# Start of an attention and two-layer kernel: the written order of blocks 0 and 1, with the queue of a store and the buffers of an output

## The chip, the cores and the metric

The kernel runs on one core of one Trainium2 chip. The metric is the time of one execution in microseconds (us); lower is better.

## The reference

All arrays are of 32-bit floats but the weights, which come as 64-bit floats.

```python
def _attn_ref(q, k, v):                    # [8, 8, 576, 64] each
    k_p = k.reshape(B, H, Sp, pool, D).mean(axis=3)   # pool = 8: 72 keys
    v_p = v.reshape(B, H, Sp, pool, D).mean(axis=3)
    scores = scale * np.matmul(q, k_p.transpose(0, 1, 3, 2))
    scores = scores - np.max(scores, axis=-1, keepdims=True)
    attn = np.exp(scores)
    attn = attn / (np.sum(attn, axis=-1, keepdims=True) + 1e-09)
    return np.matmul(attn, v_p)

x = attn_out.transpose(0, 2, 1, 3).reshape(4608, 512)
h = np.maximum(x @ w_in, 0.0)              # w_in 512 x 2048, w_out 2048 x 512
x = h * h @ w_out
h = x @ w2_in
out = np.maximum(0.01 * h, h) @ w2_out
```

## The kernel before, in words

**Tiles.** The 4608 tokens are worked in nine blocks of T = 512. A block's first product has FC = 16 chunks of 128 of the 2048 inner columns, its second product four result tiles (KC = 4 of 128 columns). Phase 0 runs attention and the first pair of weights over all blocks and leaves the result in DRAM (x2); phase 1 runs the second pair. A product is done in three passes, with each factor as the sum of two 32-bit terms: high by high, high by low, low by high. So one chunk of a first product is 4 x 3 = 12 matrix products of 512 columns.

**Weights.** A matrix of weights comes in pieces n = 0 to 15 of 1 MB (0 to 7 of w_in, 8 to 15 of w_out; each w_in piece makes two chunks). `w1.load(n)` (L268, on SP's queue) brings the 64-bit words. `w1.do(letter, n)` then turns them into the two terms, in five steps: a, the exponents (ScalarE, L218); b, the first bits (VectorE, L222 and L225); c, the low term (VectorE, L236 and L239); d, the high term (VectorE L280, and a ScalarE copy, L283); e, the low rest (VectorE, L287).

**The start.** `start()` walks a list of words, START: K, Q and V load keys, queries and values, i loads a weight piece, a to e are the conversion steps, q, k, s, n, p, x, v, m and w are attention steps (transpose of queries, pooled keys, scores with their exponentials, normalization, transpose of the probabilities, pooling of block 1's keys, pooling of values, their split, their placing). Then the values of block 0 are multiplied (L687 to L690).

**First products of blocks 0 and 1** (`first_products`, 32 units u, 16 per block). A unit multiplies one chunk into one of four PSUM banks in turn (L850), converts a weight piece (`conversion`, a piece per two units), takes relu and square on ScalarE (L860, L861) and stores the result to a DRAM buffer, `mid` (L1038). Units 0 to 15 also hold the attention of block 1, dealt out by `second_attention`: lists pe[u] of what is written ahead of a unit's products and dve[u] of what is written behind its relu (normalization L610 to L613, copies of a remainder L621, transposes of probabilities L644 and L650, their splitting L654 and L663, values L672 and L673). `loads_of(u)` deals out the loads. Results of block 0 go through tiles "r" (three buffers); those of block 1 through a ring of pieces of xh and xl.

**Second products of blocks 0 and 1** (`second_products`, 32 units). The stored results are read back six units ahead (`mid_load`, L1048), split into two terms on VectorE (`in_parts`, L866 and L867) and multiplied (L893) into the four banks. The last two pieces of w_out, n = 14 and 15, are converted here, and the attention of block 2 is dealt out among the units. At a block's end `finish` copies the four banks to tiles in turn by ScalarE (L910, m = 0 and 2) and VectorE (L908, m = 1 and 3), and SP stores them (L911).

**The other blocks** run one after the other (`run`): first products, relu, second products of one block, with the next block's attention between.

The order on every engine is the order in which the code is written. DMAs on SP's queue are issued in written order, and a DMA waits, ahead of those behind it, for what it needs. The buffers of a kind are handed out in turn: "r", "st" and "raw" have three, "gh" and "gl" two.

Of the kernel before, what the change touches and what calls it, by code (L numbers as in the profile page):

```python
# [43 lines left out]
def attention_relu2_leaky_kernel(  # L44
# [12 lines left out]
    nc = tc.nc  # L57
    B, H, S, D = q.shape
    NT, DM = out.shape
# [10 lines left out]
    T = 512  # L70
# [3 lines left out]


    START = (
        "K0 Q0 Q1 Q2 Q3 V0 i0 K1 i1 i2 Q4 Q5 i3 "
        "q0 q1 k0 s0 q2 s1 q3 n0 s2 v0 n1 s3 p0 m0 n2 p1 x1 n3 a0 b0 p2 c0 w0 d0 p3 a1 e0"
    ).split()

    pool = ctx.enter_context(tc.tile_pool(name="sb", bufs=1))
# [548 lines left out]
    def p_products(i, blk, t0):  # L630

        s = sc.pop(i)[0]
        flat = s.rearrange("p h k -> p (h k)")
        if blk not in pt:
            pt[blk] = (
                sb([P, NP, T], F32R, "pth"),
                sb([P, NP, T], F32R, "ptl"),
                sb([P, 2, T], F32R, "ptr"),
            )
        ph, pl, pr = pt[blk]  # L640
        o = i * P - t0
        ps = bank()
        for cc in range(NP):
            nc.tensor.transpose(  # L644
                ps[:, cc * P : (cc + 1) * P], flat[:, cc * PAIR : cc * PAIR + P], ident
            )

        pr_ps = bank()
        for g in range(2):
            nc.tensor.transpose(  # L650
                pr_ps[:RROWS, g * P : (g + 1) * P], prems[i % 2][:, g, :], ident
            )
        view = ps.rearrange("p (c t) -> p c t", c=NP)
        nc.scalar.copy(ph[:, :, o : o + P], view)  # L654
        last = pr_ps[:, : 2 * P].rearrange("p (c t) -> p c t", c=2)
        nc.scalar.copy(pr[:RROWS, :, o : o + P], last[:RROWS])
        low = slice(4 * REM, RROWS)

        def rest():
            for out, src in ((pl, view), (pr[low], last[low])):  # L660
                at = out[:, :, o : o + P]
                hi = ph if out is pl else pr[low]
                nc.vector.tensor_tensor(  # L663
                    out=at, in0=src, in1=f32(hi[:, :, o : o + P]), op=ALU.subtract
                )

        return rest
# [36 lines left out]
    def load_q(i):  # L704
        if i in first_tiles:
            load_home(("q", i), q_load(i))
        else:
            load_to(("q", i), q_load(i), "raw")
# [191 lines left out]

    def finish(ph, t0, acc):

        tags = ("st", "raw") if ph or t0 + T == NT else ("st", "st")
        to = x2[:, t0 : t0 + T] if ph == 0 else out[t0 : t0 + T, :]
        for m in range(KC if ph == 0 else T // P):
            st = sb([P, T if ph == 0 else DM], F32, tags[m % 2])
            if m % 2:
                nc.vector.tensor_copy(st, acc[m])  # L908
            else:
                nc.scalar.copy(st, acc[m])  # L910
            nc.sync.dma_start(out=to[m * P : (m + 1) * P, :], in_=st)  # L911
# [55 lines left out]
    def second_attention():  # L967


        pe, dve = [[] for _ in range(FC)], [[] for _ in range(FC)]  # L970
        blk, b = 1, 1
        dve[0] += [pooled_late[0], lambda: k_mask(b)]
        pe[1].append(lambda: k_transpose(b))

        def both(u, fn):
            pe[u].append(lambda: dve[u].extend(fn()))

        for j, i in enumerate(range(T // P, 2 * T // P)):
            u = 1 + 3 * j
            pe[u].append(lambda i=i: (q_transpose(i), taken(("q", i))))  # L980
            both(u + 1, lambda i=i: score_products(i))
            dve[u + 2].append(lambda i=i: normalize(i))
            both(u + 3, lambda i=i: [p_products(i, blk, T)])
        for n, (what, c) in enumerate([("v", c) for c in range(NP)] + [("rem", c) for c in range(2)]):
            both(5 + n, lambda what=what, c=c: [v_tile_pe(b, what, c)])
        dve[11].append(lambda: v_split(b))
        turn = value_steps(blk, T)
        pe[12].append(turn[0])

        def placed():  # L990
            built.add(b)
            v_place(b)

        pe[13].append(placed)
        pe[15].append(turn[1])
        return pe, dve

    def loads_of(u):

        if u == 1:  # L1000
            for c in range(NP):
                load_to(("v", 1, c), v_load(1, c), ("st", "st", "st", "gh")[c])
            for c in range(2):
                load_to(("rem", 1, c), rem_load(1, c), "gl")
        if u in (5, 8):
            load_q(6 + (u == 8))
        if u % 2 == 0 and 4 + u // 2 < FC - 2:
            w1.load(4 + u // 2)

    def conversion(u):  # L1010

# [8 lines left out]
    def first_products():  # L1020
        pe, dve = second_attention()
        for u in range(2 * FC):
            blk, c = divmod(u, FC)
            for fn in pe[u] if blk == 0 else ():
                fn()
            ps = first(blk, c)
            if u < 2 * FC - 6:
                conversion(u)
            if u == FC:
                ring.extend(t[:, i] for t in x_tiles(dt=F32) for i in range(KC))  # L1030
            r = ring[c % len(ring)] if blk else sb([P, T], F32, "r")
            relu2(r, ps)
            if u % 2 == 0 and u < 2 * FC - 8:
                w1.do("a", u // 2 + 2)
            for fn in dve[u] if blk == 0 else ():
                fn()
            loads_of(u)
            nc.sync.dma_start(out=mid[blk, c], in_=r)  # L1038
            if blk and c >= FC - AHEAD:
                mid_load(c - FC + AHEAD)  # L1040

# [8 lines left out]
    def second_products():  # L1050
        steps, turn = all_steps[2], value_steps(2, 2 * T)
        n_units, done = 2 * FC, 0
        for n in (FC - 2, FC - 1):
            w1.load(n)
        load()
        g = in_parts(mids.pop(0))
        for u in range(n_units):
            blk, c = divmod(u, FC)
            if c == 0:
                acc = [acc_bank(m) for m in range(KC)]  # L1060
            mid_load(u + AHEAD)
            if u + 1 < n_units:
                g_next = in_parts(mids.pop(u + 1))
            if u >= n_units - 2:
                turn.pop(0)()
            second(0, c, acc, g)
            for n in (FC - 2, FC - 1):
                at = u - 2 * (n - FC + 2)
                if 0 <= at < 3:
                    w1.do(("a", "bc", "de")[at], n)  # L1070
            upto = len(steps) * (u + 1) // (n_units - 2)
            while done < min(upto, len(steps)):
                steps[done]()
                done += 1
            if u >= FC // 2:
                w2.tick()
            if c == FC - 1:
                finish(0, blk * T, acc)
            g = g_next
# [69 lines left out]
```

## Time and profile before

| | us |
|---|---|
| median of three runs | 1848.42 |
| the three runs | 1848.19, 1848.42, 1849.64 |
| the profiled execution | 1846.85 |
| its span in the profile | 1845.1 |

Of the span TensorE (PE) is busy 1756.7 us (95%), VectorE (DVE) 942.5 (51%), ScalarE (ACT) 517.5 (28%). The chain of work that ended last lies to 86% on PE. The mean granted clock of PE is 0.977 of full speed. In the page's 40 slices of 46 us, PE's busy tenths begin 5 7 7 8 7 8 8 and are 9 from the eighth slice on.

The rows below have these forms. A row of waits names the waiting engine, tile and line, then the engine, tile and line that ended the wait, then the total in us, how often, and the longest. A row of a timeline has start and length in us, engine, line, operation, what is written and read, and in brackets the idle time of the engine just before and what ended it. A row of windows has the stretch, its length, each engine's busy us with its number of instructions, the granted clock (1.00 is full speed), the share of the DMA engines in use, and GB/s.

### The profile page before, as it was taken

What the parts mean: (1) busy time and instruction counts of PE and PEld (TensorE: products, weight loads), DVE (VectorE), ACT (ScalarE), POOL (GpSimd) and SP (SyncE); (2) the same over time, 40 slices, a digit from 0 to 9 for tenths busy, and PEclk for the clock granted to TensorE, in tenths of its full rate; (3) what the DMA queues carried; (4) which work ended last, traced back from release to release, by engine and by line L of the source; (5) the groups of instructions that cost most, each with busy time, mean ns of one, the idle gap of its engine ahead of it and who ended that gap; (6) DMA issues with size and microseconds to landing.
All of it is one profiled execution on the core that took longest, in us unless ns stands there. A gap on an engine that the chain in (4) does not pass through costs nothing.

```text
span 1845.1 us, 20649 instructions
## 1 busy us (share of the span) xinstructions
PE 1756.7 (95%) x8024; PEld 1454.6 (79%) x8024; DVE 942.5 (51%) x1687; ACT 517.5 (28%) x1283; POOL 0.7 (0%) x5
## 2 busy tenths in 40 slices
PE   5778788999999999999999999999999999999999
PEld 4666567888878888888888888888888888888887
DVE  6666476766766667676442234343434343434333
ACT  3455411333344343433342211111111111111111
POOL 0000000000000000000000000000000000000000
PEclk9789898999999999999999999999999999999999
DMA  8343544232323223232005511010101010101000
GB/s 233 111 137 117 185 140 158 94 100 93 100 83 114 92 92 125 86 108 92 29 1 205 204 47 46 1 46 1 46 1 46 1 46 1 46 1 46 0 24 23
DMA packets 97633, 144.01 MB, mean 78 GB/s; under 512 B 42624, under 2 KB 42752, under 8 KB 95488
## 3 DMA queue, kind: packets, MB, share of 16 engines
q1 hardware_dynamic: 97536, 142.70, 23.4%
q8 instruction: 63, 1.03, 0.2%
q14 instruction: 34, 0.28, 0.0%
HBM read 98.64 MB, written 44.04 MB: 77 GB/s over the span
## 4 chain that ended last, share of the span: by engine, by line
PE 86%; DVE 8%; ACT 3%; DMA 1%; issue 1%; SPq 1%; DVEq 0%; ACTq 0%
PE acc L893 40%; PE ps L850 38%; PE acc L850 2%; PE ps L578 2%; PE ps L545 1%; DVE val L225 1%; PE ps L644 1%; DVE val L280 1%; DVE xl L673 0%; DVE gl L867 0%; PE ps L688 0%; DMA raw<-in_q 0%; DVE val L222 0%; DMA wo<-in_v 0%; PE ps L687 0%
## 5 line engine op out<-in xcount | busy, mean ns | idle before, releaser
L850 PE MATMUL ps<-xh,wi 128*128 128x512 f32 x2048 | 673.9, 391 | 0.0
L850 PEld LDWEIGHTS ps<-xh,wi 128*128 128x128 f32 x2048 | 384.7, 188 | 79.6 <-issue 0.2
L850 PE MATMUL ps<-xl,wi 128*128 128x512 f32 x1024 | 398.8, 389 | 0.0
L876 DVE SCALAR_TENSOR_TENSOR r<-r 128x512 f32<-128x512 f32 x144 | 99.7, 693 | 461.6 <-ACT r L875 461.6
L893 PE MATMUL acc<-gh,wo 128*128 128x512 f32 x1152 | 300.1, 399 | 12.8 <-DVE st L908 7.0
L893 PE MATMUL acc<-wo,gh 128*128 128x512 f32 x1152 | 288.9, 389 | 0.0
L875 ACT COPY r<-ps 128x512 f32<-128x512 f32 x144 | 84.5, 587 | 655.6 <-PE ps L850 655.6
L893 PEld LDWEIGHTS acc<-gh,wo 128*128 128x128 f32 x1152 | 216.0, 191 | 60.1 <-DVE st L908 8.2
L893 PEld LDWEIGHTS acc<-wo,gh 128*128 128x128 f32 x1152 | 216.3, 188 | 44.9
L850 PEld LDWEIGHTS ps<-xl,wi 128*128 128x128 f32 x1024 | 192.4, 188 | 39.1
L866 DVE CAST gh<-r 128x512 fp32r<-128x512 f32 x256 | 109.2, 427 | 220.7 <-ACT r L861 206.4
L867 DVE TENSOR_TENSOR gl<-r,gh 128x512 fp32r<-128x512 f32 x256 | 177.3, 692 | 21.8 <-DVE gh L866 0.9
L893 PE MATMUL acc<-gl,wo 128*128 128x512 f32 x576 | 160.4, 393 | 0.0
L893 PE MATMUL acc<-wo,gl 128*128 128x512 f32 x576 | 158.3, 389 | 0.0
L860 ACT ACTIVATE r<-ps 128x512 f32<-128x512 f32 x112 | 67.7, 605 | 234.1 <-PE ps L850 234.1
L893 PEld LDWEIGHTS acc<-gl,wo 128*128 128x128 f32 x576 | 109.3, 190 | 23.4
L893 PEld LDWEIGHTS acc<-wo,gl 128*128 128x128 f32 x576 | 108.1, 188 | 22.5
L599 ACT ACTIVATE s<-ps,m 128x72 f32<-128x72 f32 x256 | 75.3, 328 | 120.1 <-DVE m L590 120.0
L861 ACT ACTIVATE r<-r 128x512 f32<-128x512 f32 x128 | 80.9, 632 | 4.1
L850 PE MATMUL acc<-wo,wi 128*128 128x512 f32 x192 | 48.7, 415 | 9.3 <-ACT xl L860 5.2
L850 PEld LDWEIGHTS acc<-wo,wi 128*128 128x128 f32 x192 | 38.5, 203 | 19.4 <-ACT xl L860 6.0
L850 PE MATMUL acc<-xh,wi 128*128 128x512 f32 x128 | 48.3, 444 | 0.0
(141 smaller groups left out, 1324.2 us busy)
## 6 DMA issues: line engine op xcount, KB each, us to landing
w2p<-val SPq DMA_DIRECT2D x32, 512.0 KB
pth<-x SPq DMA_DIRECT2D x9, 1024.0 KB
x<-st SPq DMA_DIRECT2D x34, 256.0 KB
wi<-in_moe_w_in SPq DMA_DIRECT2D x8, 1024.0 KB
wo<-in_moe_w_out SPq DMA_DIRECT2D x8, 1024.0 KB
val<-in_moe_w_in SPq DMA_DIRECT2D x16, 512.0 KB
val<-in_moe_w_out SPq DMA_DIRECT2D x16, 512.0 KB
wi<-w2p SPq DMA_DIRECT2D x8, 1024.0 KB
```

Of the source, the lines that this page charges most:

```text
L225: nc.vector.scalar_tensor_tensor(out=val, in0=top, scalar=0x80000000, in1=val, op0=ALU.bitwise_and, op1=ALU.bitwise_or,)
L280: nc.vector.tensor_tensor(out=w, in0=w, in1=f32(st["low"]), op=ALU.add)
L578: nc.tensor.matmul(ps[: r0 + n, c2 * PAIR : (c2 + 1) * PAIR], lhsT=qt[:, cc, : r0 + n], rhs=kts[b][:, keys], start=True, stop=True,)
L599: nc.scalar.activation(out=s[:, g, :], in_=ps[:, h * SP : (h + 1) * SP], func=AF.Exp, bias=m[:, g : g + 1], accum_out=None if i in early e ...
L850: nc.tensor.matmul(ps, lhsT=w[:, kc], rhs=x[:, kc, :], start=(kc == 0 and n == 0), stop=(kc == KC - 1 and n == 2),)
L860: nc.scalar.activation(out=r, in_=ps, func=AF.Relu)
L861: nc.scalar.activation(out=r, in_=r, func=AF.Square)
L866: nc.vector.tensor_copy(gh, r)
L867: nc.vector.tensor_tensor(out=gl, in0=r, in1=f32(gh), op=ALU.subtract)
L875: nc.scalar.copy(r, ps)
L876: nc.vector.scalar_tensor_tensor(out=r, in0=r, scalar=0.01, in1=r, op0=ALU.mult, op1=ALU.max)
L893: nc.tensor.matmul(acc[m], lhsT=w[:, piece] if ph == 0 else x[:, piece], rhs=x if ph == 0 else w, start=(c == 0 and n == 0), stop=(c == FC ...
```

## The change

Six edits, all in the order or place of work that the kernel does already.

- START is written anew: piece 0 is loaded behind Q0, ahead of Q1 to Q3 and V0; the keys' pooling and piece 0's conversion come between the score steps.
- `finish` in phase 0 (but for the last block) copies m = 0 and 2 to "st" tiles and m = 1 and 3 to "r" tiles; before, all four went to "st".
- The transposes of block 1's probabilities stand one unit later.
- The exponents of piece u/2 + 2 (step a) are written ahead of the unit's other conversion steps and of its relu; before, behind its relu.
- Loads: the queries' tiles 6 and 7 at units 2 and 5, not 5 and 8; weight pieces 4 and 5 at unit 0, 6 to 9 at units 2 to 8, 10 to 13 at units 10 to 16; before, one piece per two units, n = 4 + u/2.
- `mid` is stored from ScalarE's queue (L1040), not SP's. The last two pieces are converted in units 4 to 6 and 7 to 9 of the second products, not in 0 to 2 and 2 to 4.

```diff
     START = (
-        "K0 Q0 Q1 Q2 Q3 V0 i0 K1 i1 i2 Q4 Q5 i3 "
-        "q0 q1 k0 s0 q2 s1 q3 n0 s2 v0 n1 s3 p0 m0 n2 p1 x1 n3 a0 b0 p2 c0 w0 d0 p3 a1 e0"
+        "K0 Q0 i0 Q1 Q2 Q3 V0 i1 K1 i2 Q4 Q5 i3 "
+        "q0 k0 a0 s0 q1 b0 s1 q2 c0 n0 s2 q3 n1 s3 d0 p0 a1 n2 v0 p1 m0 e0 n3 p2 x1 w0 p3"
     ).split()
...
-        tags = ("st", "raw") if ph or t0 + T == NT else ("st", "st")
+        tags = ("st", "raw" if ph or t0 + T == NT else "r")
...
-            both(u + 3, lambda i=i: [p_products(i, blk, T)])
+            both(u + 4, lambda i=i: [p_products(i, blk, T)])
...
-        if u in (5, 8):
-            load_q(6 + (u == 8))
-        if u % 2 == 0 and 4 + u // 2 < FC - 2:
-            w1.load(4 + u // 2)
+        if u in (2, 5):
+            load_q(6 + (u == 5))
+        for n in {0: (4, 5), 2: (6,), 4: (7,), 6: (8,), 8: (9,)}.get(u, ()):
+            w1.load(n)
+        if u >= 10 and u % 2 == 0 and u // 2 + 5 < FC - 2:
+            w1.load(u // 2 + 5)
...
             ps = first(blk, c)
+            if u % 2 == 0 and u < 2 * FC - 8:
+                w1.do("a", u // 2 + 2)
             if u < 2 * FC - 6:
                 conversion(u)
...
             relu2(r, ps)
-            if u % 2 == 0 and u < 2 * FC - 8:
-                w1.do("a", u // 2 + 2)
...
-            nc.sync.dma_start(out=mid[blk, c], in_=r)
+            nc.scalar.dma_start(out=mid[blk, c], in_=r)
...
             for n in (FC - 2, FC - 1):
-                at = u - 2 * (n - FC + 2)
+                at = u - 4 - 3 * (n - FC + 2)
                 if 0 <= at < 3:
                     w1.do(("a", "bc", "de")[at], n)
```

From about line 1010 on the lines of the changed kernel stand two further down: `mid` is stored in L1040 and read back in L1050.

On ScalarE, in the first products of block 1, the rows before were these; L283 is the copy that ends a piece's step d, L218 the next piece's step a.

```order
L283 CAST wo_1185<-val 128x1024
L860 ACTIVATE xh<-acc_1169 128x512
L861 ACTIVATE xh<-xh 128x512
L218 ACTIVATE wo_1071<-wo_1071 128x1024
L860 ACTIVATE xh<-acc_1193 128x512
L861 ACTIVATE xh<-xh 128x512
L283 CAST wo_1229<-val 128x1024
```

At the same place in the changed kernel they are:

```order
L218 ACTIVATE wo_1009<-wo_1009 128x1024
L283 CAST wo_1188<-val 128x1024
L860 ACTIVATE xh<-acc_1171 128x512
L861 ACTIVATE xh<-xh 128x512
L1040 DMA mid<-xh 128x512
L860 ACTIVATE xh<-acc_1193 128x512
L861 ACTIVATE xh<-xh 128x512
L1040 DMA mid<-xh 128x512
L218 ACTIVATE wo_1073<-wo_1073 128x1024
```

L218 moved from behind the relu to ahead of L283, and two DMA issues per piece joined the queue.

On SP, in the first products of block 0, the loads of the first w_out pieces and the stores stood like this, with what each waits for (DMAHW0 to DMAHW7 are counters that the DMAs use in turn, each waiting for the DMA before it on its counter):

```order
L186 DMA raw<-in_q 128x8x64 [waits DMAHW7_49,PE_49]
L268 DMA wo_815<-in_moe_w_out 128x2x1024 [waits DMAHW0_49]
L1038 DMA mid<-r 128x512 [waits DMAHW1_49,Activation_49]
L1038 DMA mid<-r 128x512 [waits DMAHW2_49,Activation_49]
L268 DMA wo_898<-in_moe_w_out 128x2x1024 [waits DMAHW3_49,DVE_49]
L1038 DMA mid<-r 128x512 [waits DMAHW4_49,Activation_49]
L1038 DMA mid<-r 128x512 [waits DMAHW5_49,Activation_49]
L268 DMA wo_1007<-in_moe_w_out 128x2x1024 [waits DMAHW6_49]
```

In the changed kernel SP's rows there are:

```order
L186 DMA raw<-in_q 128x8x64 [waits DMAHW0_49,PE_49]
L268 DMA wo_721<-in_moe_w_out 128x2x1024 [waits DMAHW1_49]
L268 DMA wo_817<-in_moe_w_out 128x2x1024 [waits DMAHW2_49,DVE_49,Activation_49]
L268 DMA wo_888<-in_moe_w_out 128x2x1024 [waits DMAHW3_49]
L268 DMA wo_1009<-in_moe_w_out 128x2x1024 [waits DMAHW4_49]
L268 DMA wo_1073<-in_moe_w_out 128x2x1024 [waits DMAHW5_49]
L268 DMA wo_1148<-in_moe_w_out 128x2x1024 [waits DMAHW6_49]
```

The stores are gone from between the loads, and six loads of pieces 8 to 13 stand one behind the other. The stores of units 3 to 8 stand on ScalarE's queue now and use the counters of these six loads, one each, so that each of them waits for its load to land.

## Rows read from the trace of the kernel before

**Rows 1.** Windows: the stretches of the start, first and second products, and the rest.

```profile
0.00:13.50 13.50, 4.71 (x18) 3.82 (x19) 5.48 (x7) 3.15 (x5) 0.73 (x5) 1.00 0.99 244
...
54.38:155.98 101.60, 78.15 (x351) 64.78 (x350) 69.32 (x102) 54.54 (x117) 0.00 (x0) 0.83 0.40 131
155.98:214.20 58.22, 48.87 (x195) 38.79 (x194) 33.94 (x35) 27.68 (x41) 0.00 (x0) 0.91 0.36 125
...
277.00:291.50 14.50, 9.53 (x28) 7.51 (x29) 4.78 (x11) 3.04 (x17) 0.00 (x0) 0.54 0.36 124
342.50:1845.10 1502.60, 1488.73 (x6802) 1234.34 (x6800) 716.19 (x1322) 383.59 (x965) 0.00 (x0) 1.00 0.19 62
```

**Rows 2.** Waits of PE, 0 to 50 us.

```profile
PE ps L687 <- ACT pth L654: 6.7, 1, 6.7
```

**Rows 3.** Waits of DVE, 54.38 to 155.98 us.

```profile
DVE val L222 <- ACT wi L218: 22.4, 6, 5.3
DVE wo L673 <- ACT wo L672: 5.9, 3, 3.7
DVE val L222 <- ACT wo L218: 1.9, 1, 1.9
```

**Rows 4.** Lines of DVE, 54.38 to 155.98 us: busy us and mean ns, then idle before.

```profile
L239 DVE SCALAR_TENSOR_TENSOR wi<-wi 128x1024 f32<-128x1024 uint32 x7 | 8.6, 1227 | 0.2
L280 DVE TENSOR_TENSOR val<-val,wi 128x1024 f32<-128x1024 f32 x7 | 8.6, 1226 | 0.2
L225 DVE SCALAR_TENSOR_TENSOR val<-wi,val 128x1024 uint32<-128x1024 uint32 x7 | 8.6, 1225 | 0.2
L287 DVE TENSOR_TENSOR wi<-val,wi 128x1024 fp32r<-128x1024 f32 x7 | 8.5, 1218 | 0.0
L222 DVE TENSOR_SCALAR val<-wi 128x1024 uint32<-128x1024 uint32 x7 | 4.9, 693 | 22.4 <-ACT wi L218 22.4
L236 DVE TENSOR_SCALAR wi<-val 128x1024 uint32<-128x1024 uint32 x7 | 4.8, 688 | 0.1
```

**Rows 5.** Waits of PE, 52.9 to 156.32 us.

```profile
PE ps L644 <- DVE s L613: 12.5, 4, 4.7
```

**Rows 6.** Waits of SP's queue, 54 to 156 us.

```profile
SPq L1038 <- ACT r L861: 94.7, 13, 25.1
```

**Rows 7.** DMA issues, 0 to 340 us: number, size of one.

```profile
wi<-in_moe_w_in SPq DMA_DIRECT2D x8, 1024.0 KB
```

**Rows 8.** Timeline of ACT, 165 to 176 us.

```profile
171.63 1.05 ACT L283 CAST wo<-val 128x1024 fp32r<-128x1024 f32 x1 [5.12 <-DVE val L280]
...
173.74 1.13 ACT L218 ACTIVATE wo<-wo 128x1024 f32<-128x1024 f32 x1
```

**Rows 9.** Timeline of PE, 156.3 to 216 us.

```profile
156.32 16.48 PE L850 MATMUL acc<-wo,wi 128*128 128x512 f32 x72
...
201.76 12.61 PE L850 MATMUL acc<-wo,wi 128*128 128x512 f32 x48 [3.77 <-ACT xh L860]
```

**Rows 10.** Waits of PE, 214.2 to 342.6 us.

```profile
PE acc L893 <- DVE st L908: 7.0, 2, 4.8
PE acc L893 <- DVE gh L866: 5.5, 5, 2.4
PE ps L545 <- DMA raw<-in_q: 5.5, 1, 5.5
```

**Rows 11.** Timeline of DVE, 274 to 286 us.

```profile
283.30 0.69 DVE L908 COPY st<-acc 128x512 f32<-128x512 f32 x1 [6.20 <-DMA x<-st]
```

**Rows 12.** Timeline of SP's queue, 212 to 218 us.

```profile
212.97 0.32 SPq L1038 DMA_DIRECT2D mid<-xl  x1
...
217.54 0.46 SPq L186 DMA_DIRECT2D raw<-in_q  x1
```

**Rows 13.** Page, costliest groups, whole span: splitting of a chunk on DVE.

```profile
L866 DVE CAST gh<-r 128x512 fp32r<-128x512 f32 x256 | 109.2, 427 | 220.7 <-ACT r L861 206.4
L867 DVE TENSOR_TENSOR gl<-r,gh 128x512 fp32r<-128x512 f32 x256 | 177.3, 692 | 21.8 <-DVE gh L866 0.9
```

## The prediction

> **What bounds the kernel now.** I first read the windows by stage [rows 1]. From 342.5 us on PE is busy 1488.73 of 1502.60 us at full clock, so there is at most 13.9 us to win in that stretch, and the edits touch it only at the block ends. Ahead of it PE is far from full: in the first products of block 0 (54.38 to 155.98) it is busy 78.15 of 101.60 us at a clock of 0.83, in those of block 1 48.87 of 58.22 us, and around the end of block 0's second products (277 to 291.5) 9.53 of 14.50 us at 0.54. So the question is what each of these stages waits for, and I went through the waits of the engines there, stage by stage, then through the timelines around the longest.
>
> *Block 0's first products.* Here VectorE sets the pace, not by its work (69.32 of 101.60 us) but by its waits: 22.4 + 1.9 us for an exponent, L222 behind ScalarE's L218 [rows 3]. The timeline of ScalarE shows the pattern, from the stage after but the same code: ScalarE stands 5.12 us at the copy L283, which waits for VectorE's step d; then come relu and square; only then, at 173.74, the next exponent [rows 8]. VectorE has finished d by then and cannot begin the next piece. The two engines take turns. One piece costs VectorE 0.69 + 1.23 + 0.69 + 1.23 + 1.23 + 1.22 = 6.3 us [rows 4], so eight pieces are 50 us of the 69.
>
> *Block 1's first products.* The same alternation, seen from PE: it waits for relus to free a bank, as the 3.77 us before 201.76 [rows 9].
>
> *Second products.* PE waits 7.0 us for VectorE's output copies, 5.5 for splits and 5.5 for a query load [rows 10].
>
> **The change, part by part.**
>
> *Start (0 to 54.38).* The same work in another order; piece 0 arrives ahead of Q1 to Q3 and its conversion fills VectorE between score steps. What PE waits for at the end of the start is a copy of the probabilities, 6.7 us [rows 2], which now stands behind less conversion work. That is the most to be won. The most to be lost is the 1.05 MB that are put ahead of the queries: at the 244 GB/s of the first 13.5 us, where the DMA engines are full [rows 1], 4.3 us. The conversion done meanwhile covers much of that. I take **-4**, nearer to the wait, with -6.7 and +4.3 as ends.
>
> *Exponent ahead of the other steps.* In block 0 VectorE's 24.3 us of waits for exponents [rows 3] go: ScalarE now has the next exponent done before it stands at L283. What is late next is VectorE itself, with 101.6 - 24.3 = 77.3 us, the 5.9 us for L672 [rows 3] still in it. PE's busy 78.15 us are at a clock of 0.83, so they shrink if it is fed better, and don't bind at once.
>
> *Transposes of the probabilities a unit later.* PE's waits for the normalization, 12.5 us [rows 5], go or become waits for converted weights. PE isn't the bound in this stage, so: 0.
>
> *Stores from ScalarE, loads sooner.* SP's queue stood 94.7 us at stores that waited for a square, with loads behind them [rows 6]. Yet no exponent of this stage waited for a load (the waits of VectorE all end at ScalarE [rows 3]), so loads that come sooner are worth 0 here. The Trainium skill ("DMA: Bandwidth & Descriptors", section "Issuing engines are not separate DMA queues") says that starting DMAs from several engines only saves the issuing time; by it the move is worth 16 x 0.32 us of SP's issues, which the trace shows as hidden, and the 94.7 us are a matter of written order that the rule doesn't speak of.
>
> The cost is on ScalarE: 16 issues of some 0.32 us [rows 12] are 5.1 us, beside 54.54 busy of 101.6 [rows 1], so in slack. And each store is a wait in ScalarE's queue: it needs the DMA before it on its counter. For units 3 to 8 these are the six loads of pieces 8 to 13. Behind a held store stand relus, exponents and the copies that VectorE needs. By unit 8 some 24 MB must have moved: 14 pieces of 1.05 MB [rows 7], 7 MB of keys, queries and values, 8 stores of 0.26 MB. At 244 GB/s [rows 1] that is 98 us; unit 8 is due at about 50 + 8 x 5.2 = 92 us if the stage takes 82 us. So a few us are lost there, and some to exponents that stand behind a relu or a copy. I take 5 us for new waits, between 0 and 20 (nearly the 24.3 us given back); I lean low because the rates meet so nearly. Net of the stage **-19**, ends -24 and -4.
>
> *Block 1's first products.* A unit of 12 products takes 16.48 / 6 = 2.75 us when PE isn't held [rows 9]; sixteen are 44 us, the stage (156.3 to 214.2) has 57.9: **-14**. VectorE's five remaining pieces are 5 x 6.3 = 31.4 us and don't bind. If the waits of PE went but the rest of its stretching stayed, its busy 48.87 us [rows 1] would remain: -9, the other end.
>
> *Outputs in two kinds of buffer.* VectorE's copy for m = 3 waited 6.20 us for an earlier store to land [rows 11], since four copies shared three tiles; "r" tiles are free there. PE's longest wait there, 4.8 us, goes [rows 10]. Behind it PE ran at 0.54: 9.53 us busy are 9.53 x 0.54 = 5.1 at full clock, 4.4 more than needed [rows 1]; half of that lies behind the wait, -2.2. Together -7. The other 2.2 us of the waits for L908 (7.0 - 4.8) come from work ahead of it on VectorE and stay. At the later block ends the relus of the next block get their "r" tile when such a store has landed; PE is full there, and I take 0.
>
> *Last two pieces later.* The query load was issued at 217.54, behind a store [rows 12]; without stores on SP it goes out sooner, and I take -2 of the 5.5 us [rows 10]. But before, the conversions of the last two pieces ran in that wait. In units 4 to 9 VectorE now has two pieces, 12.6 us, six splits of 0.43 + 0.69 us [rows 13], 6.7 us, and some 2 us of pooling: 21 us where PE needs 6 x 2.75 = 16.5. With two buffers each for the split terms VectorE can't run far ahead, so PE waits some 5 us more for splits. Second products in all: -7 - 2 + 5 = **-4**, ends -9 (all hidden) and 0.
>
> **Sum.** -4 - 19 - 14 - 4 = -41. The profiled execution took 1846.85 us, 1.57 below the median: 1805.9 us against it, and **1807** against the median.
>
> **Rivals.**
>
> 1. *ScalarE's queue becomes the chain of block 0.* Stores held for weight loads stop relus and exponents behind them, or the exponent itself stands too late behind copies that wait. For it: ScalarE already stood 5.12 us at one instruction with a ready relu behind it [rows 8], and the loads are due within 6 us of the stores. The Trainium skill ("PSUM — Partial Sum Buffer", section "Engine vs sequencer instructions") calls ScalarE's queue strict FIFO; by that rule, the trace agrees, a store that waits holds all behind it. Against it: ScalarE has 47 us of idle time in the stage. The stage gives back 12 to 20 us more: about 1822. Chance 0.2.
> 2. *All of it lands.* Start -6.7, block 0 -24.3, block 1 -14, second products -9: -54, 1794. For it: each was a wait with one visible cause. Chance 0.14.
> 3. *The alternation only changes place.* VectorE then waits for something else on ScalarE, such as L283, L672 or the normalization's copies, and only the output copies and part of block 1 are won: -7 to -10, about 1839. Against it: nothing in the waits but L218 is large. Chance 0.05.
> 4. *Slower: the loads come so late that the stores hold everything.* One mechanism: the store of unit 8 waits for piece 13. The other stages win 22 us. To be slower by 3.7 us, block 0 must lose its 19 and 26 more, so that unit 8 comes at 92 + 45 = 137 us; that needs 24 MB at 175 GB/s or less. The trace moves 244 GB/s where the queue is full, though its stage averages are 131 and 125 [rows 1], with the queue held by stores. Some 1852. Chance 0.03.
>
> The change does what it says, by the order on the engines; a case in which it does nothing I leave out.
>
> **How the numbers follow.** The forecast has 0.58. Its own range comes from the ends: start -6.7 to 0, block 0 -24 to -12, block 1 -14 to -9, second products -9 to 0, which rarely fall together: about 1797 to 1820. The range reaches down to the second rival and up past the first: **1793 to 1827**; the third and fourth rival and the tails are the 2 in 10 left out. A measurement can tell 0.2%, 3.7 us. Faster: all but the fourth rival and a sliver, 0.94; within: 0.02; slower: 0.04.
>
> **What would show it.** Right: in block 0's first products no wait of L222 for L218 beyond the first, and the stage near 82 us with VectorE busy over 80%; block 1's at 44 to 47 us with PE above 95%; no 6 us before L908; first values of block 0 on PE near 43.5 us. Wrong: waits of ScalarE's queue at L1040 that end at a DMA from in_moe_w_out, with VectorE's L222 still waiting; a start that ends after 54 us because Q1 to Q3 come late; splits (L866) ending over 10 us of PE's waits.

## The result, and the profile after

| | before | changed |
|---|---|---|
| median, us | 1849.03 (4 runs, 1848.19 to 1850.4) | 1816.43 (4 runs, 1814.56 to 1818.87) |
| profiled execution, us | 1846.85 | 1816.79 |
| its span, us | 1845.1 | 1815.0 |

The ratio is 0.9824, with a 95% interval of 0.9807 to 0.9841: 32.6 us faster, where 41 were forecast. The profiled executions differ by 30.1 us.

To see where they came off, both spans are cut at the same four events on PE: the first L850 of block 0, the first of block 1, the first L893, the first L850 of block 2. (The prediction's first border, 54.38 us, lay a little inside block 0's stage; from here on the borders are these events.) The windows of the kernel before, with the columns of [rows 1]:

```profile
52.96:156.32 103.36, 79.91 (x359) 66.21 (x357) 70.83 (x103) 55.13 (x118) 0.00 (x0) 0.83 0.39 129
156.32:214.20 57.88, 48.53 (x193) 38.53 (x192) 33.60 (x35) 27.68 (x41) 0.00 (x0) 0.91 0.36 126
214.20:342.50 128.30, 109.13 (x495) 88.66 (x494) 89.97 (x169) 28.54 (x98) 0.00 (x0) 0.93 0.46 150
```

And those of the changed kernel:

```profile
48.96:142.16 93.20, 76.73 (x358) 63.50 (x357) 70.92 (x103) 55.38 (x118) 0.00 (x0) 0.85 0.39 143
142.16:185.68 43.52, 43.52 (x193) 36.04 (x192) 33.27 (x35) 29.16 (x41) 0.00 (x0) 1.00 0.32 111
185.68:313.52 127.84, 110.56 (x494) 89.08 (x493) 89.97 (x169) 28.50 (x98) 0.00 (x0) 0.93 0.47 153
313.52:1815.00 1501.48, 1487.25 (x6802) 1232.74 (x6800) 715.69 (x1322) 384.07 (x965) 0.00 (x0) 1.00 0.19 62
```

| stage | before | changed | difference | forecast |
|---|---|---|---|---|
| start, to the first L850 of block 0 | 52.96 | 48.96 | -4.0 | -4 |
| first products of block 0 | 103.36 | 93.20 | -10.2 | -19 |
| first products of block 1 | 57.88 | 43.52 | -14.4 | -14 |
| second products of both | 128.30 | 127.84 | -0.5 | -4 |
| rest | 1502.60 | 1501.48 | -1.1 | 0 |

Two terms came as forecast. In block 1 PE now works without a pause: its busy time is the whole stage, at full clock, and the timeline has it in one row.

```profile
142.16 43.68 PE L850 MATMUL acc<-wo,wi 128*128 128x512 f32 x192
```

The miss is in block 0 first of all. The waits of VectorE there (48.96 to 142.16 us), in the form of [rows 3]:

```profile
DVE l L610 <- ACT s L599: 7.4, 3, 3.3
DVE wo L673 <- ACT wo L672: 5.3, 3, 3.1
DVE vp L519 <- ACT vh L507: 2.2, 1, 2.2
DVE m L590 <- PE ps L578: 1.7, 2, 0.9
DVE vp L385 <- PE ps L375: 1.7, 2, 0.9
DVE val L222 <- ACT wi L218: 1.3, 1, 1.3
```

The wait of L222 for the exponent has fallen from 24.3 us [rows 3] to 1.3. In its place VectorE waits for exponentials of the scores (L610 for L599), a wait that the kernel before did not have. PE's waits in the same stage lead to a part of its cause:

```profile
PE ps L375 <- DVE ptl L663: 7.4, 2, 4.6
PE ps L443 <- DVE r L429: 5.2, 1, 5.2
PE ps L687 <- DVE ptl L663: 3.7, 1, 3.7
```

The wait of L644 for L613 [rows 5] is gone, but L375, the pooling of block 1's values, now waits 7.4 us for VectorE's L663, the splitting of the transposed probabilities. The longest of them in the timelines of VectorE, PE and ScalarE, one after the other:

```profile
77.22 1.23 DVE L225 SCALAR_TENSOR_TENSOR val<-wi,val 128x1024 uint32<-128x1024 uint32 x1
78.36 1.22 DVE L287 TENSOR_TENSOR wi<-val,wi 128x1024 fp32r<-128x1024 f32 x1
79.83 0.69 DVE L663 TENSOR_TENSOR ptl<-ps,pth 128x512 fp32r<-128x512 f32 x1 [0.26 <-ACT pth L654]
```

```profile
80.58 2.08 PE L375 MATMUL ps<-st,cst 128*128 128x128 f32 x8 [4.60 <-DVE ptl L663]
```

```profile
86.57 0.60 ACT L860 ACTIVATE r<-acc 128x512 f32<-128x512 f32 x1 [6.50 <-PE acc L850]
```

```profile
89.55 0.75 DVE L610 TENSOR_REDUCE l<-s 128x8 f32<-128x576 f32 x1 [3.32 <-ACT s L599]
```

VectorE comes to L663 after a weight piece's steps b and e. Until then PE stands 4.60 us at L375, the unit's products come later, ScalarE waits 6.50 us for them with its relu, the exponentials stand behind that relu in ScalarE's queue, and VectorE waits 3.32 us for the exponentials. The three engines hold each other up in a ring. In the code, the transposes of one tile's probabilities (two PSUM banks), the next tile's scores (two) and a value pooling (one) stand in one unit now, u = 5 and 8; `bank()` has four.

In the second products PE's waits are these:

```profile
PE acc L893 <- DVE gh L866: 7.8, 7, 2.5
PE ps L545 <- DMA raw<-in_q: 6.2, 1, 6.2
PE acc L893 <- DVE r L908: 2.2, 1, 2.2
```

Against [rows 10], the wait for output copies (L908) fell from 7.0 to 2.2 us as forecast, that for splits (L866) rose from 5.5 to 7.8, and that for the query load did not fall but rose, 5.5 to 6.2.

### The profile page after: what moved, and what is told of

The parts are those of the page before. It is cut to its first block, busy times and chain, and to the rows that moved or that the text cites. A ratio compares the mean times of both kernels' runs of the same rounds, so it can differ in the third digit from the quotient of the medians.

```text
span 1815.0 us, 20631 instructions
## 1 busy us (share of the span) xinstructions
PE 1749.8 (96%) x8024; PEld 1449.0 (80%) x8024; DVE 941.7 (52%) x1687; ACT 519.7 (29%) x1283; POOL 0.7 (0%) x5
## 4 chain that ended last, share of the span: by engine, by line
PE 89%; DVE 6%; ACT 2%; issue 1%; DMA 1%; SPq 0%; ACTq 0%; DVEq 0%
PE acc L893 41%; PE ps L850 38%; PE acc L850 4%; PE ps L578 2%; PE ps L545 1%; PE ps L644 1%; PE ps L375 1%; ACT s L599 1%; PE ps L689 0%; PE ps L688 0%; DVE xl L673 0%; PE ps L690 0%; DMA raw<-in_q 0%; DVE val L280 0%; DVE gl L867 0%
## 5 line engine op out<-in xcount | busy, mean ns | idle before, releaser
L850 PE MATMUL ps<-xh,wi 128*128 128x512 f32 x2048 | 673.7, 391 | 0.0
L850 PEld LDWEIGHTS ps<-xh,wi 128*128 128x128 f32 x2048 | 384.4, 188 | 79.6 <-issue 0.2
L850 PE MATMUL ps<-xl,wi 128*128 128x512 f32 x1024 | 398.6, 389 | 0.0
L893 PE MATMUL acc<-gh,wo 128*128 128x512 f32 x1152 | 301.1, 400 | 10.2 <-DVE gh L866 7.8
L893 PE MATMUL acc<-wo,gh 128*128 128x512 f32 x1152 | 288.9, 389 | 0.0
L893 PEld LDWEIGHTS acc<-gh,wo 128*128 128x128 f32 x1152 | 216.1, 191 | 58.1 <-DVE gh L866 9.8
L893 PEld LDWEIGHTS acc<-wo,gh 128*128 128x128 f32 x1152 | 216.2, 188 | 44.9
L866 DVE CAST gh<-r 128x512 fp32r<-128x512 f32 x256 | 109.2, 427 | 228.0 <-ACT r L861 213.8
L850 PEld LDWEIGHTS ps<-xl,wi 128*128 128x128 f32 x1024 | 192.4, 188 | 39.1
L893 PE MATMUL acc<-gl,wo 128*128 128x512 f32 x576 | 160.5, 393 | 0.0
L893 PE MATMUL acc<-wo,gl 128*128 128x512 f32 x576 | 158.3, 389 | 0.0
L893 PEld LDWEIGHTS acc<-gl,wo 128*128 128x128 f32 x576 | 109.8, 191 | 23.9
L893 PEld LDWEIGHTS acc<-wo,gl 128*128 128x128 f32 x576 | 108.2, 188 | 22.5
L599 ACT ACTIVATE s<-ps,m 128x72 f32<-128x72 f32 x256 | 75.7, 331 | 115.4 <-DVE m L590 115.4
L550 ACT COPY qt<-ps 128x512 f32<-128x512 f32 x32 | 18.8, 587 | 105.1 <-PE ps L545 105.0
L599 ACT ACTIVATION_READ_ACCUMULATOR s<-ps,m 128x1 f32 x224 | 48.3, 216 | 0.0
L850 PE MATMUL acc<-xh,wi 128*128 128x512 f32 x128 | 47.3, 435 | 0.0
```

The costliest lines, as they stand in the source:

```text
L550: nc.scalar.copy(qT[i].rearrange("p c t -> p (c t)"), ps)
L599: nc.scalar.activation(out=s[:, g, :], in_=ps[:, h * SP : (h + 1) * SP], func=AF.Exp, bias=m[:, g : g + 1], accum_out=None if i in early e ...
L850: nc.tensor.matmul(ps, lhsT=w[:, kc], rhs=x[:, kc, :], start=(kc == 0 and n == 0), stop=(kc == KC - 1 and n == 2),)
L866: nc.vector.tensor_copy(gh, r)
L893: nc.tensor.matmul(acc[m], lhsT=w[:, piece] if ph == 0 else x[:, piece], rhs=x if ph == 0 else w, start=(c == 0 and n == 0), stop=(c == FC ...
```

## The experiments

Each kernel was timed beside the kernel before. The stages are those of the table above, from the profiled execution of each.

| kernel | time, us | ratio to before, 95% interval | start | block 0 | block 1 | second products |
|---|---|---|---|---|---|---|
| before | 1849.03 | 1 | 52.96 | 103.36 | 57.88 | 128.30 |
| changed | 1816.43 | 0.9824 (0.9807 to 0.9841) | 48.96 | 93.20 | 43.52 | 127.84 |
| e1_p_early | 1812.64 | 0.9807 (0.9793 to 0.9822) | 47.07 | 88.66 | 43.64 | 128.58 |
| e2_v_units | 1807.63 | 0.9778 (0.9763 to 0.9793) | 48.81 | 84.49 | 43.52 | 126.52 |
| e3_exp_late | 1841.97 | 0.9968 (0.9955 to 0.9981) | 49.66 | 105.62 | 57.72 | 127.86 |
| e4_pieces_old | 1810.53 | 0.9794 (0.9777 to 0.9810) | 47.51 | 93.11 | 43.52 | 123.87 |
| e5_tags_old | 1821.55 | 0.9859 (0.9841 to 0.9877) | 47.84 | 93.10 | 43.53 | 134.07 |
| e6_start_old | 1821.87 | 0.9862 (0.9844 to 0.9880) | 52.78 | 93.29 | 43.52 | 127.62 |
| e7_store_sp | 1815.11 | 0.9826 (0.9809 to 0.9843) | 49.44 | 93.12 | 43.52 | 127.43 |
| e8_loads_old | 1818.30 | 0.9839 (0.9825 to 0.9854) | 48.19 | 92.62 | 43.52 | 127.62 |
| e9_v_pieces | 1804.67 | 0.9771 (0.9749 to 0.9793) | 49.16 | 84.54 | 43.52 | 122.96 |
| e10_v_qload | 1801.25 | 0.9752 (0.9734 to 0.9769) | 49.36 | 84.66 | 43.52 | 119.80 |
| e11_v_qload_spread | 1797.28 | 0.9731 (0.9714 to 0.9747) | 48.19 | 85.02 | 43.52 | 112.01 |
| e12_exp_alone | 1820.93 | 0.9850 (0.9833 to 0.9866) | 52.99 | 88.25 | 43.51 | 130.19 |

Block 0's stage repeats closely where its code is the same (93.10 to 93.29 in the changed kernel, e4, e5 and e6). Second products of the same code spread by 2 us when the stage ahead differs (126.52 in e2, 128.58 in e1), the start by 2.6 us with one code (47.07 to 49.66), and the rest, in all kernels, lies between 1501.3 and 1503.4 us. Each kernel's stages are those of one execution; the executions of one kernel differ by 1 to 7 us.

### Transposes in their old unit

```diff
-            both(u + 4, lambda i=i: [p_products(i, blk, T)])
+            both(u + 3, lambda i=i: [p_products(i, blk, T)])
```

> The changed kernel with the transposes of block 1's probabilities back in their old unit (u + 3). Stages by the first products of block 0, of block 1, of the second products and of block 2: 4.0, 10.2 and 14.4 us came off in the changed kernel, where 4, 19 and 14 were forecast. Theory A (banks): one unit later, these transposes stand in the same unit as the next tile's scores and a value pooling; two, two and one bank are asked of four, so PE stands 7.4 us at L375 for VectorE's L663, and through PE the relus, the exponentials and VectorE's L610. Undone, the waits at L375 go to under 1 us, the old waits at L644 (12.5 us before) come back in part, and block 0's stage goes from 93.2 to 87 to 92 us, the time to 1810 to 1816. Rival B (VectorE is simply full and the place makes no difference): the stage stays within 1 us of 93.2. Rival C (the later place was worth its wait): L644's waits come back in full and the stage gets longer, 96 to 102 us.

Block 0's stage is 88.66 us, 4.5 less than in the changed kernel; L375 has no wait left, and PE's first row of waits is again the old one, at half its size:

```profile
PE ps L644 <- DVE s L613: 6.7, 4, 2.4
```

So the later place cost time; rivals B and C fall. VectorE's wait of L610 for L599 stays at 5.9 us, though (7.4 in the changed kernel), so the ring over the banks accounts for only a part of it. By the times alone the two kernels can't be told apart, their intervals overlap; the stage tells it.

### Value poolings out of the crowded units

```diff
-            both(5 + n, lambda what=what, c=c: [v_tile_pe(b, what, c)])
+            both((3, 4, 6, 7, 9, 10)[n], lambda what=what, c=c: [v_tile_pe(b, what, c)])
```

> The changed kernel with the value poolings of block 1 in units 3, 4, 6, 7, 9 and 10, not 5 to 10: none is in a unit that holds transposes of probabilities and scores (5, 8, 11). Theory A (banks): the waits of L375 for L663 (7.4 us) go, relus follow sooner, VectorE's wait of L610 for L599 (7.4 us) shrinks by half or more; block 0's stage goes from 93.2 to 84 to 89 us, the time to about 1809 to 1812. Rival B (VectorE full or other waits next): the stage gets shorter by less than 2 us.

This is the sharper trial: the later transposes stay and only their company goes. The stage falls to 84.49 us, 8.7 less. In its trace these waits are left of the ring, on PE and on VectorE:

```profile
PE ps L375 <- DVE ptl L663: 0.4, 2, 0.2
```

```profile
DVE wo L673 <- ACT wo L672: 4.6, 3, 2.4
DVE vp L519 <- ACT vh L507: 2.2, 1, 2.2
DVE l L610 <- ACT s L599: 1.8, 1, 1.8
```

L375's 7.4 us are 0.4, L610's 7.4 are 1.8, and no wait of L644 is left. PE is busy 72.36 us in it at a clock of 0.92, against 76.73 at 0.85: less standing came with a higher granted clock. Theory A holds. With the poolings elsewhere the later transposes are a gain, 84.5 against the 88.7 of e1 (which has the poolings in the old units, so the 4.2 us hold for the pair).

### The exponent back behind the relu

```diff
-            if u % 2 == 0 and u < 2 * FC - 8:
-                w1.do("a", u // 2 + 2)
             if u < 2 * FC - 6:
                 conversion(u)
...
             relu2(r, ps)
+            if u % 2 == 0 and u < 2 * FC - 8:
+                w1.do("a", u // 2 + 2)
```

> The changed kernel with the exponent (step a) back behind the relu. If the exponent's place is what won in both stages of first products: L222 waits for L218 again by 20 us or more in block 0, that stage goes to 100 to 105 us and block 1's from 43.5 to 55 to 58; the time to 1837 to 1843. If it is the stores and loads that won: the stages stay within 3 us each.

Both stages are again as long as before (105.62 and 57.72 us), and the time rises by 25.5 us. VectorE's waits in block 0's stage have the old rows again, 19.1 + 2.1 us:

```profile
DVE val L222 <- ACT wi L218: 19.1, 6, 5.3
...
DVE val L222 <- ACT wo L218: 2.1, 1, 2.1
```

### The exponent's place alone

```diff
             ps = first(blk, c)
+            if u % 2 == 0 and u < 2 * FC - 8:
+                w1.do("a", u // 2 + 2)
             if u < 2 * FC - 6:
                 conversion(u)
...
-            if u % 2 == 0 and u < 2 * FC - 8:
-                w1.do("a", u // 2 + 2)
```

This edit is on the kernel before.

> The kernel before with the exponent (step a) ahead of the other steps and of the relu, and nothing else. The transposes of the probabilities are in their old unit here. If the exponent's place alone carries both stages of first products: block 0's from 103.4 to 88 to 91 us (88.7 was measured with the transposes in the old unit and all other edits), block 1's from 57.9 to 43.5, start and second products as before (53, 128.3), the time to 1818 to 1822. If the stores' and loads' places are needed with it: exponents wait for loads behind stores on SP's queue, block 0's stage stays above 93.

It alone brings 27.6 us of the change's 32.6: 15.1 in block 0, 14.4 in block 1, with 1.9 given back in the second products. In block 0 it does better than the whole change (88.25 against 93.20 us), because its transposes stand in their old unit. It also sizes the new waits, for which the prediction took 5 us: with the waits for the exponent gone, VectorE in block 0 waits for other things.

```profile
DVE l L610 <- ACT s L599: 6.2, 3, 2.5
DVE wo L673 <- ACT wo L672: 4.9, 3, 2.7
DVE vp L519 <- ACT vh L507: 2.6, 1, 2.6
```

The second row stood before too (5.9 us [rows 3]); the other two, 8.8 us, are new. By the stage's length, of the 24.3 us that went, 24.3 - 15.1 = 9.2 came back.

### Stores on SP, and the old units of the loads

```diff
-            nc.scalar.dma_start(out=mid[blk, c], in_=r)
+            nc.sync.dma_start(out=mid[blk, c], in_=r)
```

> The changed kernel with the stores of mid back on SP's queue, in the old place between the loads. If the stores' place is worth nothing on the way (as the prediction's 0 for it, with ScalarE's 5 us of issues and the held stores as cost): each stage within 2 us of the changed kernel's 93.2, 43.5 and 127.8 us, the time within 3 us. If loads behind waiting stores come too late once the stages are shorter: exponents (L218) wait for loads, block 0's or block 1's stage gets 3 to 10 us longer.

No stage moves by as much as a us; the time is 1.3 us below the changed kernel's, within the scatter. That agrees with the Trainium skill ("DMA: Bandwidth & Descriptors", section "Issuing engines are not separate DMA queues"), by which another issuing engine saves only the issue. SP's stores again wait a long time for the squares (67.0 us for r, in the form of [rows 6]), and no stage is longer for it. The row of SP's waits, 47 to 185 us:

```profile
SPq L1040 <- ACT r L861: 67.0, 11, 20.8
```

The other kernel puts back the units of the loads, with the stores left on ScalarE:

```diff
-        if u in (2, 5):
-            load_q(6 + (u == 5))
-        for n in {0: (4, 5), 2: (6,), 4: (7,), 6: (8,), 8: (9,)}.get(u, ()):
-            w1.load(n)
-        if u >= 10 and u % 2 == 0 and u // 2 + 5 < FC - 2:
-            w1.load(u // 2 + 5)
+        if u in (5, 8):
+            load_q(6 + (u == 8))
+        if u % 2 == 0 and 4 + u // 2 < FC - 2:
+            w1.load(4 + u // 2)
```

> The changed kernel with the old units of the loads (one weight piece per two units, queries at units 5 and 8). With no store on SP's queue the order of the loads among themselves should not matter much: each stage within 1.5 us, time within 2 us. If the sooner loads were needed for the shorter stages, exponents wait for loads and a stage of first products gets over 3 us longer.

Nothing moves here either: the stages are within 0.6 us of the changed kernel's. These two edits are worth nothing in the stages, each by itself. Nor are they together in the first products: in e12 both are as in the kernel before, and block 1's stage takes 43.51 us, block 0's 88.25 (88.66 in e1, which has both, and the transposes in the same unit as e12).

### One kind of output tile, and the old START

```diff
-        tags = ("st", "raw" if ph or t0 + T == NT else "r")
+        tags = ("st", "raw") if ph or t0 + T == NT else ("st", "st")
```

> The changed kernel with all four outputs of a phase 0 block in tiles of one kind again (three tiles, four copies). If the output tiles are worth what the prediction gave them: VectorE waits about 6 us for a store at L908 in the second products, PE 7 us for L908 in place of 2.2, PE's clock falls behind it, and the second products go from 127.8 to 133 to 135 us, the time to 1821 to 1824; blocks 2 to 7 stay within 1 us together. If the stores land in time by now: within 2 us of 127.8.

The second products get 6.2 us longer. PE's waits for L908 are 7.9 us against 2.2, its busy time is 111.57 us against 110.56. In the timeline VectorE's copy for m = 3 waits for a store as in [rows 11]. The rest (1501.5 us) does not change, so the later block ends were rightly put at nothing.

```profile
260.65 0.69 DVE L908 COPY st<-acc 128x512 f32<-128x512 f32 x1 [6.76 <-DMA x<-st]
```

The next kernel has the lines of START from the kernel before, with every other edit kept:

```diff
-        "K0 Q0 i0 Q1 Q2 Q3 V0 i1 K1 i2 Q4 Q5 i3 "
-        "q0 k0 a0 s0 q1 b0 s1 q2 c0 n0 s2 q3 n1 s3 d0 p0 a1 n2 v0 p1 m0 e0 n3 p2 x1 w0 p3"
+        "K0 Q0 Q1 Q2 Q3 V0 i0 K1 i1 i2 Q4 Q5 i3 "
+        "q0 q1 k0 s0 q2 s1 q3 n0 s2 v0 n1 s3 p0 m0 n2 p1 x1 n3 a0 b0 p2 c0 w0 d0 p3 a1 e0"
```

> The changed kernel with the old list START. The first product of block 0 came at 52.96 us before and at 48.96 in the changed kernel; with other edits behind the start it came at 47.1 to 49.7. If the list is worth the 4 us forecast: 51.5 to 54 us, and the time 3 to 5 us above the changed kernel's. If piece 0 ahead of the queries costs as much as it brings, and the 4 us are scatter of the loads: within 1.5 us.

With the old list the first L850 comes at 52.78 us, as in the kernel before and in e12 (52.96 and 52.99); with the new one at 47.07 to 49.66 in eleven profiles. The old wait of [rows 2] is there again, 6.7 us; in the changed kernel it is 0.5.

### The last two pieces, and the loads of block 2

```diff
-                at = u - 4 - 3 * (n - FC + 2)
+                at = u - 2 * (n - FC + 2)
```

> The changed kernel with the last two weight pieces converted in units 0 to 2 and 2 to 4 of the second products, as before. Theory: the later place costs PE waits for splits (7.8 us against 5.5) and a lower granted clock behind the two of 2.5 us; undone, the second products go from 127.8 to 122 to 125 us, the time to 1811 to 1814. Rival: in the old place the conversion waits for loads that are issued only at the start of the stage, so splits behind it are late; the stage stays at 127 to 129, or gets longer.

The second products fall to 123.87 us, 4.0 less: the later place of the last two pieces costs about what the prediction put on it (5). PE waits 3.6 us less for splits than in the changed kernel (7.8 us there), its busy time is 0.9 us shorter (109.67 against 110.56), and 0.5 us go back at the query load. PE's waits in e4's stage:

```profile
PE ps L545 <- DMA raw<-in_q: 6.7, 1, 6.7
PE acc L893 <- DVE gh L866: 4.2, 5, 2.4
```

PE's clock was lower behind such a wait as well: in the changed kernel, behind a wait of 2.52 us, eight products took 3.37 us, against 1.98 elsewhere in the stage, and the granted clock was 0.58, near the lower of the two levels (1.2 GHz). The row of PE's timeline and the window around it:

```profile
220.97 3.37 PE L893 MATMUL acc<-gh,wo 128*128 128x512 f32 x8 [2.52 <-DVE gh L866]
```

```profile
220.90:224.40 3.50, 3.43 (x9) 2.75 (x10) 3.29 (x6) 0.00 (x0) 0.00 (x0) 0.58 0.48 124
```

The gains of the two stages should add, which the next kernel tried; its edits are those of e2 and e4 together.

```diff
-            both(5 + n, lambda what=what, c=c: [v_tile_pe(b, what, c)])
+            both((3, 4, 6, 7, 9, 10)[n], lambda what=what, c=c: [v_tile_pe(b, what, c)])
...
-                at = u - 4 - 3 * (n - FC + 2)
+                at = u - 2 * (n - FC + 2)
```

> The changed kernel with the value poolings in units 3, 4, 6, 7, 9 and 10 and the last two pieces in their old units. If the two gains are of separate stages they add: block 0's stage 84.5, second products 123 to 124, time 8.7 + 4.0 = 12.7 us below the changed kernel's, about 1803.5. If they are not separate (the poolings shift when SP's queue comes free): above 1806.

They do: 84.54 and 122.96 us.

That leaves the query load. In the changed kernel the waits of SP's queue (60 to 160 us) and its timeline show why it did not come sooner:

```profile
SPq L1050 <- DMA mid<-xh: 91.9, 1, 91.9
```

```profile
185.03 3.00 SPq L1050 DMA_DIRECT2D xl<-mid  x2
188.14 1.28 SPq L268 DMA_DIRECT2D wo<-in_moe_w_out  x2
189.48 0.73 SPq L186 DMA_DIRECT2D raw<-in_q  x1
```

With its stores gone, SP still stands at the read-backs of the stored results, L1050, for 91.9 us, and the last of them goes out only at 188.03, since they wait for late stores of block 1's results. The query load follows at 189.48, 3.8 us into the stage; before it was 217.54 [rows 12], 3.3 us into it. So its place was tried, together with the poolings of e2:

```diff
-            both(5 + n, lambda what=what, c=c: [v_tile_pe(b, what, c)])
+            both((3, 4, 6, 7, 9, 10)[n], lambda what=what, c=c: [v_tile_pe(b, what, c)])
...
             if blk and c >= FC - AHEAD:
+                if c == FC - AHEAD:
+                    all_steps.update(
+                        (i, attention_steps(i, i * T, ("raw",))) for i in range(2, BLOCKS)
+                    )
+                    load()
                 mid_load(c - FC + AHEAD)
...
-        load()
         g = in_parts(mids.pop(0))
```

> The changed kernel with the value poolings in units 3, 4, 6, 7, 9 and 10 and block 2's first loads (queries, values) issued ahead of the first read-back of a stored result, not behind the loads of the last two pieces. If PE's wait at L545 (6.2 us) comes from the place of the query load in SP's queue, it goes; the clock behind it stays up and the second products go from 127 to 118 to 121 us, time about 1800 to 1802. If something else is late there (the reads of the stored results, VectorE's splits), PE waits at L893 instead: 124 us or more.

PE's wait at L545 is gone (5.8 us in e2), and the second products are 119.80 us, 6.7 less than in e2. The largest wait left there is the one for splits; the stage's window and that row:

```profile
177.54:297.34 119.80, 108.63 (x494) 87.97 (x493) 89.92 (x169) 28.44 (x98) 0.00 (x0) 0.96 0.47 156
```

```profile
PE acc L893 <- DVE gh L866: 7.9, 7, 2.5
```

The last kernel deals out the bursts of conversion (the two edits of e10, and this one):

```diff
-                at = u - 4 - 3 * (n - FC + 2)
-                if 0 <= at < 3:
-                    w1.do(("a", "bc", "de")[at], n)
+                at = u - 3 - 4 * (n - FC + 2)
+                if 0 <= at < 5:
+                    w1.do("abcde"[at], n)
```

> The kernel with value poolings in units 3, 4, 6, 7, 9 and 10 and block 2's loads ahead of the read-backs, with the last two pieces' conversion dealt out one step a unit, in units 3 to 7 and 7 to 11, not in three bursts of units 4 to 6 and 7 to 9. If the splits are late because a burst of two steps (3 us) stands ahead of them on VectorE: PE's waits for L866 fall from 7.9 to under 4 us and the second products go from 119.8 to 115 to 117 us, time about 1797. If VectorE simply has too much in these units, the waits only move: within 1.5 us of 119.8.

The waits for splits fall from 7.9 to 4.2 us, none over 0.9, and the stage to 112.01 us in the profiled execution, below the 115 to 117 expected. The gain of 7.8 us there is more than the 3.7 of waits, for PE's busy time falls too, 108.63 to 104.46 us, at a granted clock of 1.00. But that execution is the fastest of the four (1793.47 us at a mean clock of 0.992; the others took 1796.91 to 1798.63 at 0.989 to 0.990). The medians of e10 and e11 differ by 4.0 us, about the waits alone. Whether the clock stayed full in this stage in the other three isn't shown. PE's waits in the stage and its window:

```profile
PE acc L893 <- DVE gh L866: 4.2, 8, 0.9
PE acc L893 <- DVE r L908: 2.2, 1, 2.2
```

```profile
176.73:288.74 112.01, 104.46 (x494) 84.53 (x493) 89.62 (x169) 28.51 (x98) 0.00 (x0) 1.00 0.50 167
```

At 1797.28 us this kernel beats both: 0.9731 of the kernel before (0.9714 to 0.9747), 19 us below the changed one, out of three edits to the order alone.

## Why the prediction was right or wrong

**Start, -4: right in size, in part by luck.** -4.0 between the profiles, and +3.8 when the list alone is undone (e6). The first L687 comes at 43.09 us (43.5 was forecast) and the 6.7 us of [rows 2] are 0.5. PE's wait for queries behind piece 0 (L545) grew from 8.4 to 9.0 us only. Two terms that the sum did not have nearly cancel: L644's waits for the normalization fell from 5.9 to 1.0 us, and the scores' waits for the copy of the queries (L578 for L550) are new, 6.1 us. With the old list (e6) L644 waits 5.8 us again and L578 doesn't wait for L550; what in the list causes them wasn't tried. The rows of PE's waits, of the kernel before (0 to 50 us) and of the changed one (0 to 48 us):

```profile
PE ps L644 <- DVE wo L613: 5.9, 3, 2.8
PE acc L578 <- ACT kt L447: 0.4, 1, 0.4
```

```profile
PE acc L578 <- ACT wo L550: 6.1, 3, 3.7
PE ps L644 <- DVE wo L613: 1.0, 1, 1.0
```

**Exponent ahead, block 0: the mechanism right, the step's size off.** The 24.3 us of [rows 3] went, as the step said, and came back when it was undone (e3). The term that was mis-sized is "5 us for new waits": alone the edit won 15.1 us (e12), so the new waits were 9.2, 4.2 more. And they were not those that the term had in mind. No store was seen held for a weight load; the one wait of ScalarE for a DMA in the changed kernel's stage is this row of its waits, an exponent that stands behind a store, released when an earlier store had landed:

```profile
ACT wi L218 <- DMA mid<-r: 1.7, 1, 1.7
```

What came instead was next in line on ScalarE: exponentials behind a relu (L610 for L599, 6.2 us in e12), which had been hidden behind the wait for the exponent. The working looked for the new waits among stores and exponents and passed over this one. Why L610 waits in e12 and e1, where the transposes have their old place, wasn't tried by itself; PE stands 6.9 and 6.7 us at L644 for L613 there, and in e2, where it doesn't, L610's wait is 1.8 us.

**Transposes a unit later, "PE isn't the bound in this stage, so: 0": wrong.** This is the step that failed. It priced the wait that went (12.5 us, on an engine that was not the bound) and did not ask what the transposes would meet in their new unit. They met scores and a pooling, and the ring of waits over four banks cost 4.5 us against the old place (e1), and 8.7 against the same place without the poolings (e2). Together with the new waits that is the whole miss of the stage: 4.5 + 4.2 = 8.7 us, against 19 - 10.2 = 8.8. With e2's poolings block 0's stage is 84.49 us, 18.9 below the 103.36 before: the -19 of the forecast, but by another sum, and so by luck.

**Stores from ScalarE, loads sooner, 0: right** (e7, e8). The price of held stores, though, went by 244 GB/s [rows 1], a mean over a stretch of many small packets (4306 of 5493 under 512 bytes). Later, from 59 to 69 us, the changed kernel moved 376 GB/s, by the window of that stretch, and no store of this stage was held by more than the 1.7 us above.

```profile
59.00:69.00 10.00, 10.00 (x47) 7.95 (x46) 6.88 (x9) 4.42 (x6) 0.00 (x0) 0.90 1.06 376
```

**Block 1, -14: right**, 43.52 us against the 44 worked out.

**Outputs in two kinds of tile, -7: right**, 6.2 us (e5), with the 2.2 us at L908 that were to stay. Of the two terms the wait was more (5.7 us, 4.8 in the sum) and the clock behind it less (1.0 us of PE's busy time, 2.2 in the sum).

**Last two pieces later: the +5 right, the -2 wrong.** The later conversion costs 4.0 us (e4). The query load did not come sooner: the step took the stores on SP's queue for what held it, and it was the read-backs behind them (e10). The remainder of this stage is seen in e12: with its own edits all as before, it takes 1.9 us more (130.19) once the stage ahead is shorter, PE waiting 5.8 us for the query load and 4.8 for splits. Together: 128.30 + 1.9 - 6.2 + 4.0 = 128.0, against 127.84 measured. Why those 1.9 us arise wasn't tried by itself, and they lie within what this stage spreads when the one ahead differs.

**The rivals.** The third, the alternation changing place, was given 0.05 and is in part what block 0 shows: VectorE waits for ScalarE at other lines. The first had a price (1822) nearer to the 1816.43 measured than the forecast's 1807, but not its mechanism: only 1.7 us were lost behind a store, and VectorE's wait for exponents was 1.3 us; ScalarE's order did matter, through the exponentials behind the relus.

## What to carry to other kernels

When a chain of two engines is broken by moving one step, list what stands behind it on both engines before the saved wait is booked: over a third of it was owed here to the next in line. When a step is moved, count what the unit that it moves into already asks of the shared buffers, not only the wait that it leaves; a move that is free on an engine with idle time can still close a ring over the banks. And one edit undone at a time, read stage by stage, tells differences of 4 us that the times of whole runs can't, as long as the stage repeats in other profiles and the medians don't contradict it.

## What was not expected of the hardware

DMA moved 376 GB/s from 59 to 69 us, when mostly 1 MB weight pieces were under way, against 244 over the first 13.5 us, at about the same share of busy DMA engines (1.06 and 0.99 by the profile's count): a rate taken from one mix of transfers was no price for another. And a wait could cost more than its length: behind the wait of 2.52 us above, eight products took 1.4 us longer than elsewhere, at a granted clock of 0.58. In e11's profile, where no wait for splits is over 0.9 us, the granted clock of the second products is 1.00, against 0.96 in e10's; by the medians, though, that did not add to what the shorter waits gave.
